# Half the columns of one block of the first modulation, on 40 partitions and in eight transfers of their own

## The chip, the cores and the metric

The kernel runs on one core of one Trainium2 chip. The metric is device time of one execution in microseconds (us). Five engines work side by side: TensorE (PE, with its weight loads as PEld), VectorE (DVE), ScalarE (ACT), GpSimd (POOL) and SyncE (SP), which here does nothing but issue transfers. Sixteen transfer engines (DMA) move data between the chip's memory (HBM) and the on-chip buffer of 128 partitions.

## The reference

One decode step of a transformer block with adaptive layernorm, for one token of width 640, all in float32:

```python
mod = (_silu(c) @ w_mod).reshape(c.shape[0], 6, 1, -1)
sa, ca, ga, sb, cb, gb = (mod[:, 0], mod[:, 1], mod[:, 2], mod[:, 3], mod[:, 4], mod[:, 5])
h = _layernorm(x, axis=-1) * (1 + ca) + sa
x = x + ga * _A_ref(h, A_k_cache, A_v_cache, A_wq, A_wo)
h = _layernorm(x, axis=-1) * (1 + cb) + sb
x = x + gb * _B_ref(h, B_w1, B_b1, B_w2, B_b2)
```

`_A_ref` is attention of one query over a cache: 32 heads of 192, 8192 positions. Keys and values are 32 x 8192 x 192 words each, 403 MB together, and make up nearly all that is read. `_B_ref` is a dense layer of 1536 with a squared relu. The first modulation, `sa` and `ca`, is a product of the 640 values of silu(c) with 640 x 1280 weights; without it there is no `h`, and without `h` no query.

## The kernel before, in words

**The stream.** A planner (`plan`, L50) cuts keys, values, the query weights and the output weights into 53 chunks of at most 84 x 192 = 16128 words a partition. Three buffers (`slot`, L97) take the chunks in turn; the first of them holds `wm0_t` (L113) at first, the weights of the first modulation, the first 512 columns of the query weights and the small vectors x, c, b1 and b2. After the chunks come the weights of the later modulations and of the dense layer. All loads are issued by SP, in the order of the program. `wm0_t` comes first (L114), then chunk 0 and chunk 1 (L222, L223), then chunk 2 when `wm0_t`'s buffer is free (L361), and from then on chunk n + 3 at the end of the work on chunk n (L410). A load is issued when its buffer is free. SP takes its instructions in order: one that waits holds those behind it.

**Completion.** In the built program each transfer announces its end on one of eight semaphores, which are given out in turn: the first to the eighth transfer have one each, the ninth has the first one's again. A transfer that takes a semaphore over waits until the earlier transfer with it has landed. In the kernel before the ninth transfer is chunk 7.

**The start.** When `wm0_t` has landed, DVE copies the small vectors (L117), ACT and DVE work out silu(c) (L168 to L171), and `mod` (L175) multiplies. The 640 rows of the weights are split into four groups of 160; each group is 5 blocks of 32 rows, and a group's 32 rows lie on 32 partitions. So block b of all four groups lies on 128 partitions, 2 x 640 words a block, and `mod` sums over the five blocks in one accumulator: 5 blocks x 4 matmuls (L183), each for 160 of the 640 columns of both `sa` and `ca`. The result is laid out by partition (L225), the layernorm of x follows (L232), and `query` (L235) makes the first 512 columns of the query (L246).

**A chunk** (L363 to L410): values times softmax weights on PE (L307), keys times query on DVE (L258), half of the additions on POOL (L385), sums to scores on DVE (L266), softmax where a head is complete (L277).

**The end.** The last output weights, the second modulation (`mod` again, L421), the gate, the second layernorm and the dense layer (L438, L453), and the store of 640 words (L458).

Of the kernel before, what the change touches and what calls it, by code (L numbers as in the profile page):

```python
# [8 lines left out]
F32 = mybir.dt.float32  # L9
# [4 lines left out]
P = 128  # L14
D = 640
# [4 lines left out]
G = 4  # L20
DG = D // G
FG = FF // G
KB = DG // 32
FB = FG // 32
# [12 lines left out]
WQ = KB * QC  # L37
UNIT = E * DH
EXTRA = {"o": WO, "q": WQ}
SLOT = 84 * DH  # L40
VPC = 5
LEAD_FROM = 1300
LEAD = 120
# [6 lines left out]
def plan():  # L50

    chunks, kp, vp, q, o = [], 0, 0, 1, 0
    while kp < H * NPOS or vp < H * NPOS // E:
        room, w = SLOT, []
        if o < NPAIR - 1 and 2 * (o + 1) * NPOS // E <= vp:
# [8 lines left out]
        else:  # L64
            v = VPC - 1 if kp >= LEAD_FROM else VPC
            nk = min(H * NPOS - kp, (room - v * UNIT) // DH)
# [14 lines left out]
def width(chunk):  # L81
    return chunk[1] * DH + chunk[3] * UNIT + sum(EXTRA[t] for t, _ in chunk[4])
# [3 lines left out]


@with_exitstack
def block_kernel(ctx: ExitStack, tc: tile.TileContext, kv, wm0, wm1, w1, w2, out):
    nc = tc.nc  # L90
    const = ctx.enter_context(tc.tile_pool(name="const", bufs=1))
    strm = ctx.enter_context(tc.tile_pool(name="strm", bufs=3))
# [4 lines left out]
    def slot(name):  # L97
        return strm.tile([P, SLOT], F32, tag="slot", name=name, bufs=3)

# [11 lines left out]
    nc.vector.memset(eps_t, EPS)  # L111

    wm0_t = slot("wm0_t")  # L113
    nc.sync.dma_start(wm0_t[:, :wm0.shape[1]], wm0)  # L114

    small = const.tile([P, 2 * KB + FB + KB], F32, name="small")
    nc.vector.tensor_copy(small, wm0_t[:, KB * 2 * D + WQ:wm0.shape[1]])  # L117
    x_c, c_c, bbc = small[:, :KB], small[:, KB:2 * KB], small[:, 2 * KB:]

    def columns(src, n, name, pool=const, **how):  # L120

        t = pool.tile([P, n // 32, 32], F32, name=name, **how)
        nc.vector.transpose(t.rearrange("p b r -> p (b r)"), src)
        return t
# [39 lines left out]
        return h  # L164


    e = const.tile([P, KB], F32, name="silu")
    nc.scalar.activation(e, c_c, AF.Exp, scale=-1.0)  # L168
    nc.vector.tensor_scalar(e, e, 1.0, None, op0=ALU.add)
    nc.vector.reciprocal(e, e)  # L170
# [1 line left out]

    mods = const.tile([P, 6, DG], F32, name="mods")

    def mod(first, n, w, between=lambda: None):  # L175

        ps = psum.tile([P, 512], F32, tag="q", name=f"ps_mod{first}", bufs=2)
        for b in range(KB):
            if b == 3:
                between()  # L180
            wb = w[:, b].rearrange("p (m n) -> p m n", m=n)
            for g in range(G):
                nc.tensor.matmul(ps[32 * g:32 * (g + 1), :n * DG], e[:, b:b + 1].to_broadcast([P, 32]),  # L183
                                 wb[:, :, DG * g:DG * (g + 1)], start=(b == 0), stop=(b == KB - 1))
        nc.vector.tensor_copy(mods[:, first:first + n], ps[:, :n * DG].rearrange("p (m n) -> p m n", m=n))

    def gate(m, w, steps):
# [16 lines left out]
    start = [sum(width(c) for c in PLAN[:n]) * P for n in range(len(PLAN))]  # L204

    def load(n):
        if n < len(PLAN):
            chunk_t[n] = slot(f"chunk{n}")
            m = width(PLAN[n])
            cuts = (m,) if n + 1 < len(PLAN) else ((PLAN[n][3] + 1) // 2 * UNIT, m)  # L210
            pieces = [(kv[start[n]:start[n] + P * m].rearrange("(p n) -> p n", p=P), cuts)]
        else:
            name, src, cuts = (("wm1_t", wm1, WM_CUT), ("w1_t", w1, W1_CUT), ("w2_t", w2, W2_CUT))[n - len(PLAN)]
            chunk_t[name] = slot(name)
            n, pieces = name, [(src, cuts)]
        for src, cuts in pieces:
            a = 0
            for b in cuts:
                nc.sync.dma_start(chunk_t[n][:, a:b], src[:, a:b])
                a = b  # L220

    load(0)  # L222
    load(1)  # L223
    mod(0, 2, wm0_t[:, :KB * 2 * D].rearrange("p (b n) -> p b n", b=KB))
    ma = columns(mods[:, 0:2].rearrange("p m n -> p (m n)"), 2 * DG, "ma")  # L225
    ca1 = const.tile([P, KB], F32, name="ca1")

# [7 lines left out]
    def query(u, w):  # L235
        w = w.rearrange("p (b n) -> p b n", b=KB)
        ps = psum.tile([P, 512], F32, tag="q", name=f"ps_q{u}", bufs=2)
        for b in range(KB):
            nc.tensor.matmul(ps, h1[:, b:b + 1].to_broadcast([P, P]), w[:, b], start=(b == 0), stop=(b == KB - 1))  # L239
        nc.scalar.activation(qb[:, QC * u % RING:QC * u % RING + QC], ps, AF.Copy, scale=DH ** -0.5)  # L240
# [2 lines left out]
    att_a = psum.tile([P, 512], F32, tag="att", name="att_a")  # L243
    att_s = const.tile([P, D], F32, name="att_s")
    nc.vector.memset(att_s, 0.0)
    query(0, wm0_t[:, KB * 2 * D:KB * 2 * D + WQ])  # L246

    sc = const.tile([P, SRING], F32, name="sc")

# [83 lines left out]
    def attend(i, w):  # L333
        oT = os_t.pop(i)
        w = w.rearrange("p (j n) -> p j n", j=NV)
        first, last = i == 0, i == NPAIR - 1
        oW = work.tile([P, NV, 32], F32, tag="oW", name=f"oW{i}")
        nc.scalar.activation(oW, oT[:, :, None].to_broadcast([P, NV, 32]), AF.Copy)  # L338
        for j in range(NV):
            nc.tensor.matmul(att_a[96:, :512], oT[:, j:j + 1].to_broadcast([P, 32]), w[:, j, :512],  # L340
                             start=(first and j == 0), stop=(last and j == NV - 1))
        nc.tensor.matmul(att_a[:96, :NV * (D - 512)], oW.rearrange("p j r -> p (j r)"), w[:, :, 512:],  # L342
                         start=first, stop=last)
# [19 lines left out]
    for n, (kp, nk, vp, nv, extra) in enumerate(PLAN):  # L363
# [3 lines left out]
        at = nk * DH + nv * UNIT  # L367
        wo_t = None
        for what, k in extra:
            w = t[:, at:at + EXTRA[what]]  # L370
# [10 lines left out]
        if nk:  # L381
            multiply(kt, kp, nk)
            m = nk - POOL * nk // 16
# [28 lines left out]
    wm1_t, w1_t, w2_t = chunk_t["wm1_t"], chunk_t["w1_t"], chunk_t["w2_t"]  # L412
# [5 lines left out]
        evict(h)  # L418
    turn(NPAIR - 1)
    attend(*wo_t)  # L420
    mod(2, 3, wm1_t[:, KB * D:KB * 4 * D].rearrange("p (b n) -> p b n", b=KB), gather)  # L421
    x1 = const.tile([P, DG], F32, name="x1")
    nc.vector.tensor_mul(x1, att_t[0][:, :DG], mods[:, 2])
    nc.vector.tensor_add(x1, x1, x_t)
# [11 lines left out]
    for b in range(KB):  # L436
        for g in range(G):
            nc.tensor.matmul(pf[32 * g:32 * (g + 1), :FG], hT2[:, b], w1_t[:, b, FG * g:FG * (g + 1)],  # L438
                             start=(b == 0), stop=(b == KB - 1))
# [11 lines left out]
    for b in range(FB):  # L451
        for g in range(G):
            nc.tensor.matmul(py[32 * g:32 * (g + 1), :DG], fT[:, b], w2_t[:, b, DG * g:DG * (g + 1)],  # L453
                             start=(b == 0), stop=(b == FB - 1))
# [46 lines left out]
```

## Time and profile before

| | |
|---|---|
| median of 3 runs | 1055.79 us (1055.74 to 1055.89) |
| the profiled execution | 1055.83 us, span 1054.0 us |
| DVE busy | 830.2 us, 79% |
| PE busy | 497.1 us, 47% |
| first weights (4493.5 KB) | issued at 0.74 us, 13.9 us to landing |
| first chunk (6144 KB) | issued at 1.19 us, 27.9 us to landing |
| first modulation on PE | 15.73 us to 20.74 us |
| first multiply on DVE | from 32.51 us |

The span is the part of the execution that the profiler sees, from the first instruction to the last; its times start at the span's start. A line of a view names the engine, the line of the kernel (L12), the operation, and what it writes and reads; in brackets stands how long the engine was idle before and what released it. "DMA to landing" is the time from a transfer's issue to the arrival of its last byte. Most of SP's waiting, and of every engine but the one that is late, costs nothing.

### The profile page before, as it was taken

Reading aid. Unit: us, or ns where it says so; the run is one execution under the profiler, and the core shown is the slowest. Engines: PE = TensorE matmul, PEld = TensorE weight load, DVE = VectorE, ACT = ScalarE, POOL = GpSimd, SP = SyncE. Lnnn points to the kernel's source line nnn. Section 1 sums busy time; section 2 is a strip of 40 time slices with the busy share of each in tenths; the row PEclk is TensorE's granted clock in tenths of the full one; section 3 lists DMA queues with packets and bytes.
Section 4 is the critical chain, followed back from the end, with each engine's and each line's share of the span. In section 5 each row is a group of like instructions: output and inputs, shape, how many; then the busy total and the mean of one; then the engine's idle time right before and its main releaser. Section 6 shows DMA issues by size and latency. Waiting matters only on the chain.

```text
span 1054.0 us, 5116 instructions
## 1 busy us (share of the span) xinstructions
PE 497.1 (47%) x2100; PEld 133.9 (13%) x2100; DVE 830.2 (79%) x428; ACT 43.5 (4%) x122; POOL 188.2 (18%) x57
## 2 busy tenths in 40 slices
PE   2253345565452364535354357344436346345286
PEld 1010011111110010101011011011001011011022
DVE  1798878877959969888797895999887977988822
ACT  1000000000000000000000000000000000000001
POOL 0212121121212202212121121122211211211200
PEclk9676576778666686668676577676677767768699
DMA  9999999999999999999999999999999999999997
GB/s 408 434 429 431 429 432 443 449 428 431 429 433 431 429 436 430 433 430 442 435 430 433 433 427 430 436 439 436 429 429 433 432 436 438 434 431 430 420 428 313
DMA packets 8960, 452.15 MB, mean 429 GB/s; under 512 B 997, under 2 KB 1001, under 8 KB 1129
## 3 DMA queue, kind: packets, MB, share of 16 engines
q1 hardware_dynamic: 8936, 451.83, 99.3%
q8 instruction: 16, 0.26, 0.1%
q14 instruction: 8, 0.06, 0.0%
HBM read 451.82 MB, written 0.00 MB: 429 GB/s over the span
## 4 chain that ended last, share of the span: by engine, by line
DMA 56%; DVE 30%; PE 12%; ACT 1%; issue 0%; SPq 0%; DVEq 0%
DMA chunk<-in_kv 53%; DVE chunk L258 16%; DVE sc L266 12%; PE ps_o L307 6%; PE ps_q L239 2%; DMA w_t<-in_w 2%; PE att_a L340 2%; DMA wm_t<-in_wm 1%; DVE os L321 1%; DVE om L319 1%; PE ps_mod L183 0%; PE att_a L342 0%; ACT p L290 0%; PE ps_mx L282 0%; DVE nm L284 0%
## 5 line engine op out<-in xcount | busy, mean ns | idle before, releaser
L258 DVE TENSOR_TENSOR chunk<-chunk,qb 128x8064 f32<-128x8064 f32 (+19 forms) x81 | 419.7, 5212 | 127.8 <-DMA chunk<-in_kv 122.5
L307 PE MATMUL ps_o<-chunk,p 128*32 128x512 f32 x1536 | 301.5, 747 | 70.3 <-DMA chunk<-in_kv 60.8
L266 DVE TENSOR_REDUCE sc<-chunk 128x25 f32<-128x4800 f32 (+21 forms) x109 | 333.9, 3097 | 0.4
L385 POOL TENSOR_TENSOR chunk<-chunk 128x1824 f32<-128x1824 f32 (+9 forms) x51 | 187.5, 3676 | 806.5 <-DVE chunk L258 578.5
L282 PE MATMUL ps_mx<-ident,mp 128*128 128x128 f32 x32 | 14.5, 452 | 346.8 <-DVE mp L280 346.8
L307 PEld LDWEIGHTS ps_o<-chunk,p 128*32 128x32 f32 x1536 | 68.2, 133 | 278.6 <-issue 193.1
L340 PE MATMUL att_a<-chunk,oT 128*32 128x512 f32 x96 | 65.1, 833 | 42.6 <-DVE oT L330 42.6
L239 PE MATMUL ps_q<-chunk,ln_h 128*128 128x512 f32 x110 | 66.6, 767 | 25.8 <-DMA chunk<-in_kv 25.8
L282 PEld LDWEIGHTS ps_mx<-ident,mp 128*128 128x128 f32 x32 | 5.6, 176 | 375.6 <-DVE mp L280 306.8
L290 ACT ACTIVATE p<-sc,nm 128x256 f32<-128x256 f32 x32 | 16.2, 508 | 649.6 <-DVE nm L284 649.6
L239 PEld LDWEIGHTS ps_q<-chunk,ln_h 128*128 128x128 f32 x110 | 26.7, 253 | 63.7 <-issue 34.6
L319 DVE TENSOR_TENSOR om<-ps_o,mask 96x512 f32<-96x512 f32 x32 | 21.6, 675 | 8.5 <-PE ps_o L307 8.5
L284 DVE TENSOR_REDUCE nm<-ps_mx 128x1 f32<-128x128 f32 x32 | 9.3, 292 | 19.5 <-PE ps_mx L282 19.5
L321 DVE TENSOR_REDUCE os<-om 96x64 f32<-96x512 f32 x32 | 21.8, 682 | 1.1
L340 PEld LDWEIGHTS att_a<-chunk,oT 128*32 128x32 f32 x96 | 12.2, 142 | 78.1 <-DVE oT L330 45.1
L329 DVE TENSOR_REDUCE oT<-ps_oT 128x3 f32<-128x96 f32 x16 | 4.0, 248 | 21.0 <-PE ps_oT L325 21.0
L295 PE MATMUL ps_sum<-ident,wide 128*128 128x128 f32 x16 | 7.4, 465 | 22.4 <-ACT wide L293 22.4
L183 PE MATMUL ps_mod<-wm_t,silu 128*32 128x320 f32 (+1 forms) x80 | 9.4, 621 | 15.8 <-DVE silu L171 15.7
L325 PE MATMUL ps_oT<-ident,os 96*128 96x96 f32 x16 | 5.0, 313 | 20.8 <-DVE os L321 20.8
L342 PE MATMUL att_a<-chunk,oW 128*96 128x384 f32 x32 | 14.6, 538 | 0.0
L240 ACT ACTIVATE qb<-ps_q 128x512 f32<-128x512 f32 x12 | 7.2, 597 | 137.2 <-PE ps_q L239 137.2
L338 ACT ACTIVATE oW<-oT 128x96 f32<-128x96 f32 x16 | 4.5, 280 | 177.6 <-DVE oT L330 177.6
(78 smaller groups left out, 93.6 us busy)
## 6 DMA issues: line engine op xcount, KB each, us to landing
chunk<-in_kv SPq DMA_DIRECT2D x38, 8064.0 KB, 37.2
chunk<-in_kv SPq DMA_DIRECT2D x11, 8000.0 KB, 39.0
chunk<-in_kv SPq DMA_DIRECT2D x2, 7872.0 KB, 38.5
chunk<-in_kv SPq DMA_DIRECT2D x1, 6144.0 KB, 27.9
wm_t<-in_wm SPq DMA_DIRECT2D x1, 4493.5 KB, 13.9
wm_t<-in_wm SPq DMA_DIRECT2D x1, 4480.0 KB, 27.6
chunk<-in_kv SPq DMA_DIRECT2D x1, 3264.0 KB
chunk<-in_kv SPq DMA_DIRECT2D x1, 3072.0 KB, 28.2
```

Source lines behind the costliest of these rows:

```text
L183: nc.tensor.matmul(ps[32 * g:32 * (g + 1), :n * DG], e[:, b:b + 1].to_broadcast([P, 32]), wb[:, :, DG * g:DG * (g + 1)], start=(b == 0), s ...
L239: nc.tensor.matmul(ps, h1[:, b:b + 1].to_broadcast([P, P]), w[:, b], start=(b == 0), stop=(b == KB - 1))
L258: nc.vector.tensor_mul(pr, pr, q[:, None, :].to_broadcast([P, b - a, DH]))
L266: nc.vector.tensor_reduce(sc[:, a % SRING:a % SRING + b - a], src[:, a - first:b - first], axis=AX.X, op=ALU.add)
L282: nc.tensor.transpose(ps[:, :P], mp.to_broadcast([P, P]), ident)
L290: nc.scalar.activation(p, s[:, :, None].to_broadcast([P, NPOS, 32 // E]), AF.Exp, bias=nm, accum_out=sp[:, h % 2:h % 2 + 1])
L307: nc.tensor.matmul(ps_t[h][32 * g:32 * (g + 1)], p[:, E * j:E * (j + 1)].rearrange("p e r -> p (e r)"), t[:, g], start=(j == 0), stop=last)
L319: nc.vector.tensor_mul(om[:n], ps_t.pop(h)[:n].rearrange("p (d e) -> p d e", e=E), mask[:n, None, :].to_broadcast([n, ED, E]))
L321: nc.vector.tensor_reduce(os_[:n, h % 2], om[:n], axis=AX.X, op=ALU.add)
L340: nc.tensor.matmul(att_a[96:, :512], oT[:, j:j + 1].to_broadcast([P, 32]), w[:, j, :512], start=(first and j == 0), stop=(last and j == NV ...
L342: nc.tensor.matmul(att_a[:96, :NV * (D - 512)], oW.rearrange("p j r -> p (j r)"), w[:, :, 512:], start=first, stop=last)
L385: nc.gpsimd.tensor_add(half, half, kt[:, m:, DH // 2:])
```

## The change

Block 4, the last of the five, is 2 x 640 words wide. Of it, the columns 320 to 639 of `sa` and of `ca` (`GX` = 2 of the 4 column groups, `WX` = 640 words) leave the rows of `wm0`. They lie in an array of their own, `wm0x`, of 40 rows, which go to partitions 0 to 19 and 32 to 51 (`RX` = 20). A row of it holds up to four (`SX`) pieces of 640 words: 128 rows of the block are dealt out over 40 partitions, 4 pieces on every fourth partition and 3 on the others. c is dealt out in the same way, in 4 more columns (`cx`).

The pieces come in eight transfers of five rows each, the rows of one transfer four partitions apart, 2560 words a row in the first of each four and 1920 in the others. They land at the end of the first buffer, on 64 partitions which DVE sets to zero first (partitions that hold no piece must be zero). `mod` does 18 of its 20 matmuls as before, and then 4 x 2 over 64 partitions, one for each piece and column group, with the matching column of silu(c). A row of `wm0` goes from 8987 to 8351 words (640 leave, 4 come).

In the built program the weights are the first transfer, the eight small ones the second to the ninth, and chunk 0 and chunk 1 the tenth and the eleventh. The ninth waits for the first one's semaphore. PE's first matmul on the pieces waits for all eight small transfers. Nothing else changes but the numbers of the lines.

```diff
+GX = 2
+SX = 4
+RX = 20
+WX = 2 * GX * DG
+W0 = KB * 2 * D - WX
...
     wm0_t = slot("wm0_t")
+    wm0x_t = wm0_t[:64, SLOT - SX * WX:]
+    nc.vector.memset(wm0x_t, 0.0)
     nc.sync.dma_start(wm0_t[:, :wm0.shape[1]], wm0)
+    for h in range(2):
+        for a in range(4):
+            n = WX * (SX if a == 0 else SX - 1)
+            nc.sync.dma_start(wm0x_t[32 * h + a:32 * h + RX:4, :n], wm0x[RX * h + a:RX * (h + 1):4, :n])
...
-    nc.vector.tensor_copy(small, wm0_t[:, KB * 2 * D + WQ:wm0.shape[1]])
-    x_c, c_c, bbc = small[:, :KB], small[:, KB:2 * KB], small[:, 2 * KB:]
+    nc.vector.tensor_copy(small, wm0_t[:, W0 + WQ:wm0.shape[1]])
+    x_c, c_c, bbc = small[:, :KB], small[:, KB:2 * KB + SX], small[:, 2 * KB + SX:]
...
-    def mod(first, n, w, between=lambda: None):
+    def mod(first, n, w, wx=None, between=lambda: None):
...
-            wb = w[:, b].rearrange("p (m n) -> p m n", m=n)
-            for g in range(G):
+            gs = G - GX if wx is not None and b == KB - 1 else G
+            wb = w[:, b * n * D:b * n * D + gs * n * DG].rearrange("p (m n) -> p m n", m=n)
+            for g in range(gs):
...
+        if wx is not None:
+            wx = wx.rearrange("p (s m n) -> p s m n", s=SX, m=n)
+            for s in range(SX):
+                for g in range(GX):
+                    nc.tensor.matmul(ps[32 * (G - GX + g):32 * (G - GX + g + 1), :n * DG],
+                                     e[:64, KB + s:KB + s + 1].to_broadcast([64, 32]),
+                                     wx[:, s, :, DG * g:DG * (g + 1)], start=False, stop=(s == SX - 1))
...
-    mod(0, 2, wm0_t[:, :KB * 2 * D].rearrange("p (b n) -> p b n", b=KB))
+    mod(0, 2, wm0_t[:, :W0], wm0x_t)
```

More of the change, by code (lines that the diff above doesn't have):

```diff
@@ L88, in block_kernel @@
 @with_exitstack
-def block_kernel(ctx: ExitStack, tc: tile.TileContext, kv, wm0, wm1, w1, w2, out):
+def block_kernel(ctx: ExitStack, tc: tile.TileContext, kv, wm0, wm0x, wm1, w1, w2, out):
     nc = tc.nc
@@ L113, in block_kernel @@
     wm0_t = slot("wm0_t")
+    wm0x_t = wm0_t[:64, SLOT - SX * WX:]
+    nc.vector.memset(wm0x_t, 0.0)
     nc.sync.dma_start(wm0_t[:, :wm0.shape[1]], wm0)
-    small = const.tile([P, 2 * KB + FB + KB], F32, name="small")
-    nc.vector.tensor_copy(small, wm0_t[:, KB * 2 * D + WQ:wm0.shape[1]])
-    x_c, c_c, bbc = small[:, :KB], small[:, KB:2 * KB], small[:, 2 * KB:]
+    for h in range(2):
+        for a in range(4):
+            n = WX * (SX if a == 0 else SX - 1)
+            nc.sync.dma_start(wm0x_t[32 * h + a:32 * h + RX:4, :n], wm0x[RX * h + a:RX * (h + 1):4, :n])
+    small = const.tile([P, 2 * KB + SX + FB + KB], F32, name="small")
+    nc.vector.tensor_copy(small, wm0_t[:, W0 + WQ:wm0.shape[1]])
+    x_c, c_c, bbc = small[:, :KB], small[:, KB:2 * KB + SX], small[:, 2 * KB + SX:]
     def columns(src, n, name, pool=const, **how):
@@ L164, in layernorm @@
         return h
-    e = const.tile([P, KB], F32, name="silu")
+    e = const.tile([P, KB + SX], F32, name="silu")
     nc.scalar.activation(e, c_c, AF.Exp, scale=-1.0)
@@ L245, in block_kernel @@
     nc.vector.memset(att_s, 0.0)
-    query(0, wm0_t[:, KB * 2 * D:KB * 2 * D + WQ])
+    query(0, wm0_t[:, W0:W0 + WQ])
     sc = const.tile([P, SRING], F32, name="sc")
@@ L420, in block_kernel @@
     attend(*wo_t)
-    mod(2, 3, wm1_t[:, KB * D:KB * 4 * D].rearrange("p (b n) -> p b n", b=KB), gather)
+    mod(2, 3, wm1_t[:, KB * D:KB * 4 * D], between=gather)
     x1 = const.tile([P, DG], F32, name="x1")
@@ L485 @@
           for kp, nk, vp, nv, extra in PLAN]
+    m0 = rows(wm[:, :2 * D], KB)
+    cc = column(c, KB)
+    at = [(s, 32 * h + r) for s in range(SX) for h in range(2) for r in range(RX) if s < SX - 1 or r % 4 == 0][:P]
+    xs, xp = np.array(at).T
+    xw, cx = np.zeros((P, SX, WX), np.float32), np.zeros((P, SX), np.float32)
+    xw[xp, xs] = m0[:, W0 - WX:].reshape(P, 2, D)[:, :, D - GX * DG:].reshape(P, WX)
+    cx[xp, xs] = cc[:, KB - 1]
     arrays = {
         "kv": np.concatenate(kv),
-        "wm0": np.concatenate([rows(wm[:, :2 * D], KB), wq[0], column(A_x, KB), column(c, KB),
-                               column(B_b1, FB), column(B_b2, KB)], axis=1),
+        "wm0": np.concatenate([m0[:, :W0 - WX], m0[:, W0 - WX:].reshape(P, 2, D)[:, :, :D - GX * DG].reshape(P, WX),
+                               wq[0], column(A_x, KB), cc, cx, column(B_b1, FB), column(B_b2, KB)], axis=1),
+        "wm0x": np.concatenate([xw[32 * h:32 * h + RX] for h in range(2)]).reshape(2 * RX, SX * WX),
         "wm1": np.concatenate([rows(wm[:, 5 * D:], KB), rows(wm[:, 2 * D:5 * D], KB)], axis=1),
```

## The prediction

> **What bounds the kernel now.** I read the page from the top first: the row of the sixteen transfer engines over the span, then the queues.
>
> ```profile
> span 1054.0 us, 5116 instructions
> DMA  9999999999999999999999999999999999999997
> q1 hardware_dynamic: 8936, 451.83, 99.3%
> HBM read 451.82 MB, written 0.00 MB: 429 GB/s over the span
> ```
>
> The queue that SP fills is busy for 99.3% of the span. No slice of the forty is below nine tenths but the last. The kernel is a stream of 452 MB, and its time is the time of that stream plus its two ends. The view of stretches says the same of the middle and shows the close.
>
> ```profile
> 55.00:1000.00 945.00, 443.72 (x1723) 115.08 (x1723) 788.36 (x367) 33.54 (x102) 181.60 (x50) 0.70 1.00 433
> 1040.00:1045.00 5.00, 2.37 (x32) 0.82 (x24) 2.43 (x6) 0.00 (x0) 0.00 (x0) 1.00 0.98 413
> 1045.00:1046.00 1.00, 0.60 (x20) 0.63 (x24) 0.15 (x1) 0.00 (x0) 0.00 (x0) 1.00 0.86 358
> 1047.00:1048.00 1.00, 0.24 (x8) 0.00 (x0) 0.00 (x0) 0.00 (x0) 0.00 (x0) 1.00 0.48 200
> 1049.00:1050.00 1.00, 0.74 (x24) 0.40 (x20) 0.00 (x0) 0.00 (x0) 0.00 (x0) 1.00 0.04 15
> ```
>
> The last two columns are the DMA share and GB/s. From 55 to 1000 us the share is 1.00 at 433 GB/s: nothing starves the engines. At the close the share falls over some four us, so the engines do not end together, and the last one sets the end. The chain of waits names compute as well, so I check that slots do not set the pace.
>
> ```profile
> DMA 56%; DVE 30%; PE 12%; ACT 1%; issue 0%; SPq 0%; DVEq 0%
> 45.51 10.22 DVE sc L266 x2
> 55.75 31.91 DMA chunk<-in_kv
> 1029.56 20.33 DMA w_t<-in_w
> ```
>
> The load issued at 55.75, when the scores of the first chunk free its slot, lands 31.91 us later. It is a full slot, 8064 KB, and its own bytes take 8.26 MB / 433 GB/s = 19.1 us. So 12.8 us of earlier transfers stood ahead of it. DVE's part of the chain is real, but it ends 12.8 us before the engines would run dry. A delay of the stream is thus a delay of the end. A delay of DVE is nothing until it reaches 12.8 us. The last transfer lands at 1029.56 + 20.33 = 1049.9, and only some 4 us of compute and the store follow.
>
> **The start, where the change lies.** The view in order of time (start, duration, engine, line) and the landings of the issues:
>
> ```profile
> 0.74 0.39 SPq L114 DMA_DIRECT2D wm_t<-in_wm  x1
> 1.19 31.01 SPq L219 DMA_DIRECT2D chunk<-in_kv  x3
> 1.64 0.06 DVE L111 MEMSET eps_t<- 128x1 f32 x1
> 14.62 0.18 DVE L117 COPY small<-wm_t 128x27 f32<-128x27 f32 x1 [12.92 <-DMA wm_t<-in_wm]
> 15.73 4.96 PE L183 MATMUL ps_mod<-wm_t,silu 128*32 128x320 f32 x40 [15.73 <-DVE silu L171]
> 24.47 7.38 PE L239 MATMUL ps_q<-wm_t,ln_h 128*128 128x512 f32 x10 [1.08 <-DVE ln_h L163]
> 32.51 12.96 DVE L258 TENSOR_TENSOR chunk<-chunk,qb 128x12288 f32<-128x12288 f32 x1 [5.34 <-ACT qb L240]
> chunk<-in_kv SPq DMA_DIRECT2D x1, 6144.0 KB, 27.9
> wm_t<-in_wm SPq DMA_DIRECT2D x1, 4493.5 KB, 13.9
> ```
>
> SP issues the first weights at 0.74, the first chunk right behind them at 1.19, and then the second. The weights land at 14.6 (DVE's copy runs at 14.62), the first chunk (6144 KB) at 1.19 + 27.9 = 29.1. Between the two landings 6.29 MB moved in 14.5 us: 434 GB/s. At that rate the weights' 4.60 MB are worth 10.6 us, but they took 13.9 from their issue. So a transfer that finds the engines empty pays **3.3 us of start-up** (issue, first bytes, the slowest engine's lag, the landing), and one that finds a queue pays none. This number carries the forecast.
>
> **The change part by part.**
>
> *The first transfer shrinks.* Its row goes from 8987 to 8351 words: 636 x 4 x 128 = 0.326 MB less, 0.75 us at 434 GB/s. It lands at 14.62 - 0.75 = 13.87.
>
> *Eight small transfers come behind it*, 2560 or 1920 words by five rows, 0.33 MB in all. The stream's bytes stay the same, so bytes cost nothing. The first of the eight waits for the new memset of 64 x 2560 words.
>
> ```profile
> 0.83 0.17 DVE L104 MEMSET ones<- 128x128 f32 x1 [0.83 <-PEq L494]
> 24.49 0.59 DVE L245 MEMSET att_s<- 128x640 f32 x1
> ```
>
> From 128 to 640 words a row, a memset grows by 0.42 us, 0.82 ns a word. 2560 words make 2.2 us, from 1.7 to 3.9. DVE has nothing else until 13.87, and the queue holds 0.33 MB less than 4.6 MB of work, so this is hidden. If that cover were gone it would cost 2.2 us. Between the two issues above lie 1.19 - 0.74 = 0.45 us, so seven small ones leave SP by 3.9 + 7 x 0.45 = 7.1, with the weights still under way.
>
> *The ninth transfer waits, and the chunks stand behind it.* The order of the built program gives every transfer one of eight semaphores in turn. The last small transfer is the ninth of the program and takes the first one's semaphore, so SP holds it until the weights have wholly landed. SP works in order: the first and the second chunk, which in the kernel before were issued by 1.19 and just after, are held behind it. This is a wait that the trace of before does not have, since there the ninth transfer comes long after the first. SP resumes at 13.87, issues the small one (0.45) and then the first chunk at 13.87 + 0.45 = **14.32**. By then the engines have drained: all that was queued is the weights, landed, and the seven small ones. The first chunk finds (nearly) empty engines, pays the start-up again, and lands at 14.32 + 3.3 + 14.5 = 32.1 where it landed at 29.1: **+3.0 us**, for it and everything behind it.
>
> This cost I bound from both sides. The start-up is 3.3 by the nearest row, a load over all partitions into empty engines. From below, the store at the end is the only other transfer that meets empty engines:
>
> ```profile
> 1051.47 0.65 SPq L458 DMA_DIRECT2D out_y<-y  x1
> SPq L497 <- DMA out_y<-y: 0.7, 1, 0.7
> ```
>
> It is issued for 0.65 us and waited for another 0.7: some 1.4 us for 2.5 KB on few engines. With 1.4 the sum is 14.32 + 1.4 + 14.5 - 29.1 = +1.1, with 3.3 it is +3.0. I take the nearest row's end, less a little, **+2.8**: part of the 3.3 is the lag of the slowest engine, and the close shows that the engines end four us apart, so the one that lags at the restart need not be the one that ends last. Upwards, a landing a few tenths later would add as much: up to +3.7.
>
> The Trainium skill (DMA: Bandwidth & Descriptors, section Anatomy of one DMA) gives a fixed cost of about 2.0 us for each transfer, fitted on GpSimd's path; that would make the sum +1.7, and the 3.3 us of this trace's own first load speaks for more.
>
> *The small rows' engines.* If five rows use five engines, each takes 2 x 10240 + 5 x 7680 = 58,880 bytes of the seven, 2.2 us at 434 / 16 = 27 GB/s. That ends by 13.87 + 2.2 = 16.1 at the latest, inside the start-up of the chunk (14.32 + 3.3), so it adds nothing.
>
> *More matmuls.* The modulation has 18 of the old and 8 new matmuls in place of 20; each counts twice in the row (x40), so 12 more at 4.96 / 40 = 0.124 us: +1.5 us on PE. The weights come 0.75 earlier, so the query and the first multiply move by about +0.7, to 33.2. The chunk, landing at 32.1, still comes before that. The slot then frees at some 56.5 and not 55.75, against 12.8 us of queue (and the stream is late itself), so nothing of it reaches the end. The last small transfer is issued at 13.87 and with 3.3 lands by 17.2; PE starts at 13.87 + (15.73 - 14.62) = 15.0 and reaches its rows 36 x 0.124 = 4.5 us later, at 19.5: hidden with 2.3 us to spare.
>
> *The sum.* The profiled execution took 1055.83 us, 1.8 more than its span, and the median of the runs is 1055.79, the same for this purpose. 1055.8 + 2.8 = **1058.6**.
>
> **The rivals.**
>
> *Slots absorb it.* If the loads wait for slots, and not for engines, a late stream catches up and only PE's +0.7 stays: 1056.5. For it speaks SP's own list of waits:
>
> ```profile
> SPq L219 <- DVE sc L266: 750.9, 50, 24.8
> chunk<-in_kv SPq DMA_DIRECT2D x38, 8064.0 KB, 37.2
> ```
>
> SP does wait 750.9 us for slots. Against it: the loads land 37.2 us after issue where their bytes take 19.1, so a full transfer stands ahead of each, and the share is 1.00 in the middle.
>
> *The slowest engines are unloaded.* This is the other side: not slower. The engines that carry no small row lose 0.75 us of work each, and if one of them ends last (the close runs over four us), the end comes 0.75 earlier: 1055.0. The Trainium skill (same page, sections Why a DMA increments its semaphore by 16 and not by 1, and The descriptor swizzle) says that five rows go to the five lowest engines and that partitions 0 to 19 and 32 to 51 are these engines' own, which would make this the effect; no row here names an engine. It decides only if the chunk is queued before the engines drain: by the sum above the shift is (start-up - 0.3), so the start-up would have to be under 0.3 us.
>
> *All five rows go through one engine.* Then one engine has 0.33 MB / 27 GB/s = 12 us more, the chunk's part on it starts some 10 us late, and the end with it: 1066. No row shows a five-row transfer.
>
> **How the numbers follow.** About 0.2% (2.1 us, so beyond 1057.9) is what a measurement of this kernel can tell from no change. The forecast, drained and refilled engines, has 0.80, between 1057.0 and 1059.5: 0.66 beyond 1057.9 and 0.14 short of it. Slots absorb it: 0.07. Unloaded engines: 0.06, one hundredth of that faster by over 0.2%. One engine: 0.04. What I have not thought of: 0.03, mostly slower. So slower 0.66 + 0.04 + 0.02 = 0.72, faster 0.02, within 0.2% the remaining 0.26. The bounds +1.1 and +3.7 make the range 1057.0 to 1059.5, which leaves the three rivals out.
>
> **What would show it.** In the profile after, DVE's copy of the small columns should start near 13.9; SP's first chunk issue should stand near 14.3, not 1.19, with a wait for the first weights ahead of it; the DMA share between about 14 and 16 should fall well below one; the multiply should start near 33.2 with the chunk just landed; from 55 to 1000 the share should be 1.00 again. If the chunk is issued by 8 us, the forecast is wrong and the unloaded engines are next. If the share in the middle falls below 1.00, slots do set the pace.

## The result and the profile after

| | before | after |
|---|---|---|
| median of 9 runs | 1055.79 us (1055.62 to 1056.00) | 1058.68 us (1058.49 to 1058.87) |
| ratio | | 1.0026 (95%: 1.0017 to 1.0035) |
| the profiled execution, its span | 1055.83 us, 1054.0 us | 1058.74 us, 1057.0 us |

The change costs 2.9 us, 0.26%. The forecast was 1058.6. Where the time went is read in the same order as before. First the page of the kernel after, its span, the engines' row over the span, and SP's queue:

```profile
span 1057.0 us, 5161 instructions
DMA  8999999999999999999999999999999999999997
q1 hardware_dynamic: 9016, 451.83, 99.1%
```

The bytes are the same 451.83 MB. Of the forty slices one has changed: the first, from 9 to 8. The view in order of time of the kernel after shows what happens in that slice:

```profile
2.17 2.19 DVE L120 MEMSET wm_t<- 64x2560 f32 x1 [0.48 <-issue]
4.39 9.66 SPq L125 DMA_DIRECT2D wm_t<-in_wm0x  x8
13.40 0.18 DVE L128 COPY small<-wm_t 128x31 f32<-128x31 f32 x1 [9.03 <-DMA wm_t<-in_wm]
14.09 17.65 SPq L238 DMA_DIRECT2D chunk<-in_kv  x3
14.54 4.68 PE L195 MATMUL ps_mod<-wm_t,silu 128*32 128x320 f32 x36 [14.54 <-DVE silu L182]
19.15 2.34 PE L201 MATMUL ps_mod<-wm_t,silu 64*32 64x320 f32 x16
25.25 6.13 PE L258 MATMUL ps_q<-wm_t,ln_h 128*128 128x512 f32 x10 [1.08 <-DVE ln_h L174]
32.05 12.96 DVE L277 TENSOR_TENSOR chunk<-chunk,qb 128x12288 f32<-128x12288 f32 x1 [4.09 <-ACT qb L259]
```

The first chunk is issued at 14.09 and not at 1.19. It goes out 0.69 us after the weights have landed (13.40). The eight small transfers leave SP between 4.39 and 14.05, and the one row for the eight hides a gap before the last. SP's waits in the kernel after (what it waited for: us in total, times, the longest) name that gap:

```profile
SPq L125 <- DMA wm_t<-in_wm: 3.9, 1, 3.9
SPq L125 <- DVE wm_t L120: 3.3, 1, 3.3
```

Once, SP waits for the memset, and once, for 3.9 us, for the first weights: the ninth transfer, held by the first one's semaphore. The stretches of the kernel after (the last two columns are the DMA share and GB/s; a packet is booked where it begins, so a stretch can exceed 1):

```profile
12.00:13.00 1.00, 0.00 (x0) 0.00 (x0) 0.00 (x0) 0.00 (x0) 0.00 (x0) 1.00 0.24 97
13.00:14.00 1.00, 0.00 (x0) 0.00 (x0) 0.32 (x2) 0.37 (x2) 0.00 (x0) 1.00 0.33 136
14.00:15.00 1.00, 0.46 (x4) 0.20 (x8) 0.42 (x3) 1.00 (x1) 0.00 (x0) 1.00 0.26 92
15.00:16.00 1.00, 1.00 (x12) 0.40 (x8) 0.00 (x0) 0.13 (x1) 0.00 (x0) 1.00 2.39 745
20.00:30.00 10.00, 7.01 (x24) 3.18 (x21) 4.81 (x16) 0.26 (x1) 0.00 (x0) 0.83 0.95 413
55.00:1000.00 945.00, 435.73 (x1722) 112.95 (x1722) 786.07 (x366) 33.53 (x102) 181.53 (x50) 0.71 1.00 433
```

In the kernel before, the same stretches read:

```profile
12.00:13.00 1.00, 0.00 (x0) 0.00 (x0) 0.00 (x0) 0.00 (x0) 0.00 (x0) 1.00 0.36 157
13.00:14.00 1.00, 0.00 (x0) 0.00 (x0) 0.00 (x0) 0.00 (x0) 0.00 (x0) 1.00 1.48 639
14.00:15.00 1.00, 0.00 (x0) 0.00 (x0) 0.18 (x1) 0.16 (x1) 0.00 (x0) 1.00 0.80 344
20.00:30.00 10.00, 6.98 (x23) 3.13 (x16) 4.82 (x16) 0.26 (x1) 0.00 (x0) 0.67 1.01 436
```

From 13 to 15 us the engines were at work before (1.48 and 0.80); after, they stand mostly idle (0.33 and 0.26) and the chunk's packets come in the stretch from 15 (2.39). Counted from the trace's single packets, the sixteen engines stand idle for some 32 engine-us between 12 and 16 us, 2.0 us each; in the kernel before they are never idle there. The restart is slow as well: the eight packets of the first chunk that an engine carries take 15.2 us together, where they took 14.5. The last packets of the first chunk end at 30.26 to 31.38 on the sixteen engines, where they ended at 27.56 to 28.75, 2.8 us later on the mean: 2.0 of idle engines and 0.7 of slower packets make nearly all of it. Then the share is 1.00 at 433 GB/s from 55 to 1000, as before: nothing of the delay is caught up and nothing is added, and the end comes 2.9 us later.

### The profile page after: what moved, and what is told of

It reads as the page before. It is cut to its first block, busy times and chain, and to the rows that moved or that the text cites. A ratio compares the mean times of both kernels' runs of the same rounds, so it can differ in the third digit from the quotient of the medians.

```text
span 1057.0 us, 5161 instructions
## 1 busy us (share of the span) xinstructions
PE 491.0 (46%) x2112; PEld 133.1 (13%) x2112; DVE 832.6 (79%) x429; ACT 43.5 (4%) x122; POOL 188.1 (18%) x57
## 3 DMA queue, kind: packets, MB, share of 16 engines
q1 hardware_dynamic: 9016, 451.83, 99.1%
HBM read 451.83 MB, written 0.00 MB: 427 GB/s over the span
## 4 chain that ended last, share of the span: by engine, by line
DMA 56%; DVE 31%; PE 11%; ACT 1%; issue 0%; SPq 0%; DVEq 0%
DMA chunk<-in_kv 53%; DVE chunk L277 16%; DVE sc L285 13%; PE ps_o L326 5%; PE att_a L359 2%; DMA w_t<-in_w 2%; PE ps_q L258 2%; DMA wm_t<-in_wm 1%; DVE os L340 1%; DVE om L338 1%; PE att_a L361 0%; ACT p L309 0%; PE ps_mx L301 0%; PE ps_mod L195 0%; DVE nm L303 0%
## 5 line engine op out<-in xcount | busy, mean ns | idle before, releaser
L326 PE MATMUL ps_o<-chunk,p 128*32 128x512 f32 x1536 | 296.5, 735 | 79.1 <-DMA chunk<-in_kv 69.4
L258 PE MATMUL ps_q<-chunk,ln_h 128*128 128x512 f32 x110 | 63.4, 735 | 26.4 <-DMA chunk<-in_kv 26.4
L195 PE MATMUL ps_mod<-wm_t,silu 128*32 128x480 f32 (+1 forms) x76 | 9.1, 615 | 15.2 <-DVE silu L182 14.5
L361 PE MATMUL att_a<-chunk,oW 128*96 128x384 f32 x32 | 14.5, 534 | 0.0
```

What stands on the lines that cost most here:

```text
L326: nc.tensor.matmul(ps_t[h][32 * g:32 * (g + 1)], p[:, E * j:E * (j + 1)].rearrange("p e r -> p (e r)"), t[:, g], start=(j == 0), stop=last)
```

## The experiments

The theory was that the ninth transfer's wait empties the engines and that the refill costs some 3 us, whatever the small transfers carry. The rivals were the bytes on few engines, the mere number of transfers and a late DVE. The intervals of the ratios below are some ±0.9 us wide, so two kernels less than 1 us apart are not told apart by them.

### Six or seven unread transfers in the kernel before

Into the kernel before, between the weights and the first chunk, go six (e3) or seven (e4) transfers of five rows by 128 words that nobody reads. With seven, the first chunk is the ninth transfer.

```diff
     nc.sync.dma_start(wm0_t[:, :wm0.shape[1]], wm0)
+    for i in range(6):     # e4: range(7)
+        nc.sync.dma_start(wm0_t[:5, SLOT - P * (i + 1):SLOT - P * i], wm0[:5, P * i:P * (i + 1)])
```

> The kernel before with six transfers of five rows of 512 bytes, that nobody reads, between the weights and the first chunk; the first chunk is the eighth transfer and does not wait. Theory: 1055.8, within 0.3, since the issue of the first chunk at some 4 us is still far ahead of the drained engines. Rival (small transfers cost in themselves): +0.45 us for each, 1058.5.

> The same with seven: the first chunk is the ninth transfer and waits for the weights, which land at 14.6. Theory: issue at some 14.65, 0.56 later than in the change, so the loss is 2.9 + 0.56 = 3.4 us: 1059.2 (1058.8 to 1059.6). Rival (small transfers cost in themselves): 0.45 more than with six.

Measured: e3 1056.16 us, ratio 1.0004 (0.9995 to 1.0013). e4 1059.03 us, 1.0030 (1.0019 to 1.0042), so +3.2. In order of time, e3:

```profile
1.19 2.19 SPq L116 DMA_DIRECT2D wm_t<-in_wm  x6
3.42 28.51 SPq L221 DMA_DIRECT2D chunk<-in_kv  x3
```

and e4:

```profile
1.18 2.64 SPq L116 DMA_DIRECT2D wm_t<-in_wm  x7
14.32 0.18 DVE L119 COPY small<-wm_t 128x27 f32<-128x27 f32 x1 [12.63 <-DMA wm_t<-in_wm]
14.32 18.02 SPq L221 DMA_DIRECT2D chunk<-in_kv  x3
```

In e4 the chunk's issue and the copy stand at the same 14.32: both waited for the weights. SP's waits in e4 name it:

```profile
SPq L221 <- DMA wm_t<-in_wm: 10.5, 1, 10.5
```

and the stretches of e4 show empty engines:

```profile
13.00:14.00 1.00, 0.00 (x0) 0.00 (x0) 0.00 (x0) 0.00 (x0) 0.00 (x0) 1.00 0.09 18
14.00:15.00 1.00, 0.00 (x0) 0.00 (x0) 0.37 (x3) 0.44 (x2) 0.00 (x0) 1.00 0.00 0
```

What follows: the step from six to seven transfers of 2.5 KB costs 2.9 us (1059.03 - 1056.16). Between the two neither matmuls nor a memset has changed, and of the bytes only 2.5 KB. The wait alone is enough for the whole of the change's cost, and six transfers without it cost nothing that can be measured.

### Seven unread transfers, one of them ahead of the weights

If the wait for the weights costs, and not the reuse of a semaphore as such, it must go when a tiny transfer has the first semaphore. One transfer is issued ahead of the weights, the other six behind them; they have 1, 2, 3, 4, 5 and 5 rows.

```diff
+    def mark(rows, n, at):
+        nc.sync.dma_start(wm0_t[:rows, SLOT - at - n:SLOT - at], wm0[:rows, at:at + n])
+
+    mark(5, P, 0)
     nc.sync.dma_start(wm0_t[:, :wm0.shape[1]], wm0)
+    for i, rows in enumerate((1, 2, 3, 4, 5, 5)):
+        mark(rows, P * (i + 2), P * (i + 1) * (i + 2) // 2)
```

> The kernel before with seven unread marks, as many as in the run that lost 3.2 us, but one of them ahead of the weights, and with one to five rows. The first chunk is the ninth transfer and waits for that first mark, which lands at some 2.5 us, so it is issued with the weights under way. Theory (what counts is what the wait is for): 1055.8 plus 0.4, as the weights are issued one mark later: 1056.2 (1055.9 to 1056.6). Rival (the number of transfers or the re-used semaphore itself): 1059.0 as with seven marks behind the weights.

Measured: 1057.18 us, 1.0011 (1.0003 to 1.0020), +1.3. In order of time:

```profile
3.85 12.25 SPq L225 DMA_DIRECT2D chunk<-in_kv  x2
15.76 0.18 DVE L123 COPY small<-wm_t 128x27 f32<-128x27 f32 x1 [14.06 <-DMA wm_t<-in_wm]
```

The chunk is issued at 3.85 with the engines full, so the ninth transfer now waits for nothing that is late, and 1.9 of the 3.2 us are gone. But 1.3 us stay where 0.4 was expected. The weights, issued at 1.19, land at 15.76: 15.76 - 1.19 - 10.6 of bytes leaves 4.0 us of start-up, 0.7 more than before. That and 0.45 us for the later issue would make 1.15. Why this start-up is longer is not shown.

### The change with six small transfers

The change itself, but with five pieces in the longest rows and so three transfers for each half: six in all, and the first chunk is the eighth transfer.

```diff
-SX = 4
+SX = 5
...
-        for a in range(4):
+        for a in range(3):
...
```

The array `wm0x` is filled to match.

> The change with six small transfers in place of eight (three of each four partitions, up to five pieces on a partition), so that the first chunk is the eighth transfer and waits for no semaphore; the second chunk waits for the weights with the first one queued behind them. Theory (the wait drained the engines): the first chunk's issue is back near 8 us, the engines are not idle between 13 and 15, and the 2.9 us of the change go. What stays is the moved bytes: five engines carry 1.7 us more (2.4 of small rows less 0.75), eleven 0.75 less. If one of the eleven ends last as in the rival of the prediction, 1055.0; if one of the five does, up to 1057.3. Rival (the small transfers or the matmuls themselves cost): 1058.2 to 1058.8 as the change.

Measured: 1057.37 us, 1.0015 (1.0006 to 1.0024), +1.6. In order of time the chunk leaves early and the weights land at 13.7:

```profile
9.46 4.57 SPq L238 DMA_DIRECT2D chunk<-in_kv  x2
13.70 0.18 DVE L128 COPY small<-wm_t 128x32 f32<-128x32 f32 x1 [8.67 <-DMA wm_t<-in_wm]
```

The stretches of e1 around that landing:

```profile
13.00:14.00 1.00, 0.00 (x0) 0.00 (x0) 0.18 (x1) 0.08 (x1) 0.00 (x0) 1.00 0.52 214
14.00:15.00 1.00, 0.16 (x4) 0.16 (x8) 0.56 (x3) 0.98 (x2) 0.00 (x0) 1.00 1.84 791
```

The wait ahead of the first chunk is gone and the engines do not run dry (a packet is booked where it begins, hence 0.52 beside 1.84; counted from the single packets no engine is idle between 12 and 16 us), yet half of the cost is left. It shows at the other end of the kernel, in the last stretches:

```profile
1047.00:1048.00 1.00, 1.00 (x20) 0.86 (x16) 0.00 (x0) 0.00 (x0) 0.00 (x0) 0.50 0.52 215
1048.00:1049.00 1.00, 1.00 (x23) 0.84 (x16) 0.00 (x0) 0.00 (x0) 0.00 (x0) 0.50 0.09 36
1049.00:1050.00 1.00, 1.00 (x30) 0.78 (x26) 0.00 (x0) 0.00 (x0) 0.00 (x0) 0.75 0.06 26
1050.00:1051.00 1.00, 0.98 (x32) 0.64 (x20) 0.00 (x0) 0.00 (x0) 0.00 (x0) 1.00 0.04 15
```

A share of 0.06 is one engine of sixteen, at 26 GB/s. In the kernel before the stretch from 1048 has five times that:

```profile
1048.00:1049.00 1.00, 0.62 (x20) 0.60 (x24) 0.00 (x0) 0.00 (x0) 0.00 (x0) 1.00 0.30 123
```

There several engines shared the end; here a single one works alone from 1048.4 to 1050.8. The trace does not name the engines, but each packet begins 3 or 4 ns before the end of its predecessor on the same engine. Followed so, packet by packet, it is one of the five that carry small rows. The other four end at 1046.8 to 1047.9. This one also fetches instructions: four short fetches, and each of them delays its other packets by 0.98 us, 3.9 us together. In the kernel before the engine with these four fetches ended at 1049.2 already, beside eight engines with two longer fetches each (1.5 to 1.6 us of delay for one, ends at 1047.9 to 1049.45). Its small rows put it behind all of them: it carries 2 x 12,800 + 4 x 10,240 bytes and loses 8 x 635 x 4 of the weights' rows, 46,240 bytes more, 1.7 us at 27 GB/s.

So when the stream does not stop, the bytes do cost, on one engine. When it stops, as in the change, the five engines move their small rows while the other eleven stand idle, and the price is not paid on top: 2.9 for both, 3.2 for the wait alone (in e4), 1.6 for the bytes without the wait. The first two are not told apart. The packets of the kernel after agree: the engine with the four fetches ends at 1052.2, the next one, which carries no small row, at 1052.0.

### Six small transfers, with more and with fewer bytes

Three runs vary what the engines carry. e6 has six transfers of four rows (`SX = 6`, `RX = 16`). e10 moves half the bytes (`GX = 1`, the edits of `SX` and of the loop as in e1). e2 moves all of the block's columns (`GX = 4`).

> The six small transfers with four rows in place of five (24 partitions, up to six pieces each), so that four engines carry the rows: each 3.0 us more less 0.75. In the trace of the six transfers by five rows, followed engine by engine, one of the five ends last and the other four end with some 3 us to spare, since that one also carries four short instruction fetches. If that engine is the fifth, it is spared here and the eleven others and it lose 0.75: 1055.0 to 1055.3. If it is one of the first four: 2.3 more than before, less what it has to spare: 1057.8 to 1058.1.

> The six small transfers by five rows with one column group and not two: rows half as long, so each of the five engines carries 1.2 us more less 0.37, 0.85 in place of 1.7. Theory (the five engines' bytes are what is left when the wait is gone): the excess is about half of the 1.57 us measured with two groups, 1056.4 to 1056.7. Rival (the six transfers, the memset or the matmuls): as with two groups, 1057.4.

> As the six transfers, with all four column groups of the last block and not two: the small rows are twice as long, so the five engines carry 3.3 us more and the eleven 1.5 less. Unloaded engines: 1054.3. Five engines that end last: the excess over before is twice that of the six transfers with half the block, some +3 us, 1058.9. Rival (neither matters): the same as the six transfers with half the block.

Measured: e6 1057.90 us, 1.0018 (1.0009 to 1.0027), +2.0. e10 1057.08 us, 1.0012 (1.0003 to 1.0021), +1.2. e2 1060.32 us, 1.0044 (1.0031 to 1.0056), +4.5. The close of e6:

```profile
1049.00:1050.00 1.00, 1.00 (x20) 0.85 (x16) 0.00 (x0) 0.00 (x0) 0.00 (x0) 0.50 0.05 20
1050.00:1051.00 1.00, 1.00 (x21) 0.82 (x17) 0.00 (x0) 0.00 (x0) 0.00 (x0) 0.56 0.06 26
```

and of e10:

```profile
1048.00:1049.00 1.00, 1.00 (x24) 1.00 (x19) 0.00 (x0) 0.00 (x0) 0.00 (x0) 0.50 0.05 20
1049.00:1050.00 1.00, 1.00 (x20) 0.53 (x16) 0.00 (x0) 0.00 (x0) 0.00 (x0) 0.50 0.07 31
```

In both, one engine is alone again, and it is among the loaded, in e6 too with four rows a transfer. By the working of e1, a loaded engine carries 23,200 bytes more in e10 (0.9 us), 46,240 in e1 (1.7) and 61,632 in e6 (2.3); measured were +1.2, +1.6 and +2.0. The order is right, the slope is not settled, since each pair's intervals overlap. In all three the late engine is the one with the four fetches; its last packet, at 1049.2 in the kernel before, ends at 1050.6 in e10, 1050.8 in e1 and 1051.6 in e6.

e2 does not answer what it was made for. Its order in time shows why:

```profile
2.97 5.39 DVE L121 MEMSET wm_t<- 64x6400 f32 x1 [1.27 <-issue]
8.39 4.38 SPq L126 DMA_DIRECT2D wm_t<-in_wm0x  x6
12.81 0.44 SPq L241 DMA_DIRECT2D chunk<-in_kv  x1
```

The memset is 5.39 us long and SP waits for it, six issues follow, and the chunk goes out at 12.81, after the weights have landed (12.75). The engines ran dry here too, 29.6 engine-us idle between 12 and 16 us, though no semaphore held the chunk: a memset ahead of the issues is enough when it is long. Its +4.5 us mixes this with the bytes.

### The pieces on 32 partitions, in one transfer

One transfer of 32 rows onto partitions 0 to 31 brings the same 128 pieces. There is neither a memset nor a ninth transfer.

```diff
-RX = 20
+RX = 32
...
-    wm0x_t = wm0_t[:64, SLOT - SX * WX:]
-    nc.vector.memset(wm0x_t, 0.0)
+    wm0x_t = wm0_t[:RX, SLOT - SX * WX:]
...
-    for h in range(2):
-        for a in range(4):
-            n = WX * (SX if a == 0 else SX - 1)
-            nc.sync.dma_start(wm0x_t[32 * h + a:32 * h + RX:4, :n], wm0x[RX * h + a:RX * (h + 1):4, :n])
+    nc.sync.dma_start(wm0x_t, wm0x)
...
```

> The change with its 128 pieces on 32 partitions (four each, 0 to 31) in one transfer of 32 rows, two rows for each of sixteen engines, and no memset. No wait ahead of the first chunk and no engine with more bytes than another; the eight extra matmuls stay. Theory: 1055.8, within 0.3. Rival (the matmuls, or the small rows themselves, cost): over 1056.5.

Measured: 1057.01 us, 1.0010 (1.0001 to 1.0018), +1.1 where nothing was expected, though the interval hardly separates it from nothing. The order in time has nothing late:

```profile
1.20 0.41 SPq L121 DMA_DIRECT2D wm_t<-in_wm0x  x1
1.65 30.18 SPq L234 DMA_DIRECT2D chunk<-in_kv  x3
14.06 0.18 DVE L124 COPY small<-wm_t 128x31 f32<-128x31 f32 x1 [12.36 <-DMA wm_t<-in_wm]
```

The trace's packets hold a hint. The small rows are packets of 10,240 bytes; in the change those take 0.385 us each, here 0.385 to 0.922, with a median of 0.664. At two rows for each of sixteen engines that is some 0.6 us. The first chunk's packets behind them are slower too (15.5 us an engine for 14.5), and its last ones end at 29.12 to 29.95, 1.6 us later on the mean than before, with no engine idle between 12 and 16 us. So the loss is made in the transfers at the start; in e1, which has more extra matmuls, those packets take 14.5. That many engines writing few partitions at once slow each other is a guess, and the cause of this 1.1 us stays open.

### A late DVE

In the kernel before, the memset of `att_s` that stands in front of the first multiply is repeated, 14, 20 or 25 times in all. Only DVE is late then, by 0.79 us for each memset and gap, less what it would have waited for the query.

```diff
-    nc.vector.memset(att_s, 0.0)
+    for _ in range(25):     # e9: 20, e12: 14
+        nc.vector.memset(att_s, 0.0)
```

> The kernel before with 14 memsets in place of one ahead of the first multiply, so that it starts near 37.6, some 5 us late. In the run with 20 (9.8 late) the load was issued at 65.5, the DMA rate between 65 and 70 fell to 361 GB/s, and 1.9 us were lost: so the queue ahead was not 12.8 us long but that less the start-up, 12.8 - 3.3 = 9.5. Theory (9.5 us cover a late DVE): 1055.8, within 0.4, and no dip between 60 and 70. Rival (DVE's lateness costs in proportion, 1.9 us for 9.8): 1056.8.

> The kernel before with 20 memsets in place of one ahead of the first multiply. In the run with 25 each took 0.79 us with its gap, so the multiply started at 46.45, 13.9 us late and not 9.6 as expected, past the 12.8 us of queued transfers, and the DMA share fell to 0.48 between 60 and 70 us. With 20 it starts near 42.5, 10.0 late, and the load that follows is issued 2.8 us ahead of dry engines. Theory: 1055.8, within 0.5. Rival (a late DVE costs its share from the first us): 1055.8 + 5.1 x 10.0 / 13.9 = 1059.5.

> The kernel before with 25 memsets of 0.59 us in place of one before the first multiply, which then starts near 42 and not 32.5. Theory (12.8 us of queued transfers cover a late DVE): 1055.8, within 0.4. Rival (slots set the pace): up to 9.6 us more, 1065.

Measured: e12 1055.98 us, 1.0001 (0.9992 to 1.0010); e9 1057.80 us, 1.0021 (1.0013 to 1.0030), +1.9; e8 1061.04 us, 1.0048 (1.0034 to 1.0062), +5.1. The first multiply starts at 37.48, 42.32 and 46.45 us, so 5.0, 9.8 and 13.9 late. The stretch from 65 to 70 us, in which the queued transfers come to their end and the next should follow, in e12:

```profile
65.00:70.00 5.00, 5.00 (x27) 1.65 (x28) 4.97 (x2) 0.60 (x1) 2.03 (x1) 1.00 0.95 413
```

in e9:

```profile
65.00:70.00 5.00, 4.12 (x6) 1.97 (x7) 4.34 (x4) 0.60 (x2) 0.00 (x0) 0.50 0.98 361
```

and in e8:

```profile
65.00:70.00 5.00, 0.00 (x0) 0.02 (x1) 4.83 (x3) 0.00 (x0) 0.32 (x1) 0.50 0.00 0
```

413, 361 and 0 GB/s: fed, short, and dry. A DVE that is 5 us late is free: counted from the single packets, no engine of e12 is idle between 55 and 80 us. At 9.8 late it costs 1.9 and at 13.9 late 5.1. If every us beyond the cover costs one, the cover is some 9.8 - 1.9 = 7.9 to 13.9 - 5.1 = 8.8 us. The packets give it more sharply: the engines stand idle for 0.9 us each in e9 and 5.0 us each in e8, and 9.8 - 0.9 and 13.9 - 5.0 are both 8.9.

### The price of an issue over stepped partitions

The small transfers of the change left SP more slowly than forecast. e11 is e3 with the rows four partitions apart.

```diff
-        nc.sync.dma_start(wm0_t[:5, SLOT - P * (i + 1):SLOT - P * i], wm0[:5, P * i:P * (i + 1)])
+        nc.sync.dma_start(wm0_t[:20:4, SLOT - P * (i + 1):SLOT - P * i], wm0[:5, P * i:P * (i + 1)])
```

> The six unread marks behind the weights, 512 bytes a row, on partitions 0, 4, 8, 12, 16 and not 0 to 4. In the change each small transfer held SP for 0.66 us, the marks for 0.33. If the step of the partitions makes the difference: 0.66 us each here; if the length of the rows: 0.33. The time stays that of the six marks, 1056.2 (1055.7 to 1056.6), since the first chunk is still issued by 6 us.

Measured: 1056.02 us, 1.0001 (0.9992 to 1.0010). The views of the one line (duration in ns: least, median, most; then the first and the last start) of e3:

```profile
L116 SPq DMA_DIRECT2D wm_t<-in_wm x6: 262/323/403, 1.2 to 3.0; - x6
```

of e11:

```profile
L116 SPq DMA_DIRECT2D wm_t<-in_wm x6: 657/657/856, 1.2 to 4.9; - x6
```

and of the kernel after:

```profile
L125 SPq DMA_DIRECT2D wm_t<-in_wm0x x8: 657/658/867, 4.4 to 13.4; - x8
```

Five rows on neighbouring partitions are issued in 0.32 us, five rows four partitions apart in 0.66, and the change pays the latter. In e11, and for the first seven transfers of the change, nothing of it reaches the end, since SP is ahead of the engines there.

## Why the prediction was right

*The stream sets the end.* Right. Chunk 0 is 2.8 us late on the mean engine, the end 2.9, and the share between is 1.00. The cover that the prediction put beside it, 12.8 us for a late DVE, was **too large**: e9 loses 1.9 us at 9.8 late, and by the packets the cover is 8.9. The packets show the two parts that the working missed. In the kernel before, the load issued at 55.75 begins at 65.8 on the mean engine, so the work queued ahead lasts 10.0 us and not 12.8. The 12.8 was taken from the landing at 87.66, and the slowest engine sets that: its packets end at 87.2, those of the mean engine at 84.9. And a late load, in e8 issued at 69.64, has its first packet at 70.60, 1.0 us later: 10.0 - 1.0 = 9.0. The change did not come near this bound.

*The weights shrink.* They landed at 13.40, not 13.87. Without their 9.85 us of bytes and the issue at 0.73 this leaves 2.8 us of start-up, where the first load before had 3.3.

*Memset and issues.* The memset was sized right (2.19 us for 2.2). The issues were not: 0.66 us each, not 0.45, as the nearest row had been a transfer over neighbouring partitions and e11 shows that the step makes the difference. Seven left by some 9.5 us and not 7.1; SP then still waited 3.9 us for the weights, so this did not count. The ninth, behind the landing, did count its 0.69 (with the gap) instead of 0.45.

*The ninth transfer's wait and the refill.* This is the step that carries the sum, and e3 against e4 shows it alone: nothing for six, 2.9 us for one more. e7 shows from the other side that it is the wait for the weights. The chunk's issue came at 14.09 (forecast 14.32), two errors that nearly cancel: 0.47 earlier landing, 0.24 longer issue. From there its last packet ends at 31.38, 31.38 - 14.09 - 14.5 = 2.8 us of start-up; 1.1 of it passes before the first packet (15.18). The prediction's 3.3 counts to the landing, which in the kernel before came 0.3 after the last packet (29.1 against 28.75); counted so, the restart is some 3.1, inside the bounds of 1.4 and 3.3 and close to the upper. The Trainium skill (DMA: Bandwidth & Descriptors, Anatomy of one DMA) has some 2.0 us for a transfer's fixed cost, fitted on GpSimd's path. The restart here is above it, as the prediction had held. The last tenths are luck: the step gives +2.6 on the slowest engine, the mean engine is 2.8 late and the end 2.9, so the little that the prediction took off for the slowest engine is not borne out.

*The small rows' engines: nothing.* Right for the change, but with a reason that e1 narrows. The last of them end at 15.43 (forecast 16.1 at the latest). They are hidden because the engines stand idle; in e1, where these do not, one loaded engine ends last and the small rows cost 1.6 us.

*More matmuls.* PE's part of the modulation took 4.68 + 2.34 = 7.02 us for 4.96, so +2.1 and not +1.5: the passes over 64 partitions cost 2.34 / 16 = 0.146 us and not 0.124. Yet the multiply started at 32.05, earlier than before and than the 33.2 of the forecast, as the query took 6.13 us and not 7.38; the granted clock from 20 to 30 us was 0.83 where it was 0.67. Neither reaches the end.

*The rivals.* That slots absorb it was wrong: the share in the middle is 1.00, and the end is as late as the first chunk. That all five rows go through one engine was wrong: the trace shows five packets at a time, one on each of five engines (the first five begin between 12.28 and 12.51 us). The Trainium skill (DMA: Bandwidth & Descriptors, Why a DMA increments its semaphore by 16 and not by 1) gives five rows five engines, and the trace agrees. That the unloaded engines would end earlier fell in a way that the prediction did not have. Its condition, a chunk queued before the engines drain, was met in e1, and the unloaded engines did end earlier there, the last of them at 1048.4 where it was 1049.45. Yet the time came out 1.6 us above before and not 0.75 below: the engine that ends last was one of the loaded.

No version that was run is faster than the kernel before. The best that lighter unloaded engines could give, 0.75 us or 0.07%, is less than these runs can tell from nothing.

## What to carry to other kernels

Count the transfers ahead of the first large stream: where completions share a few semaphores in turn, one small transfer more can wait for the first large one, hold everything behind it in the same queue, and empty the engines. A refill is paid once in full by a kernel that the transfers bound. Cover for a late issue is the work still queued on the mean engine, less the time from an issue to its first packet (1.0 us here); a landing overstates it. Before giving bytes to a few engines, look at the last microseconds for the engine that ends last, and see that it is not among them.

## What the runs showed of the hardware that was not expected

- A transfer over stepped partitions keeps SP for 0.66 us, one of the same size over neighbouring ones for 0.32 (e11 and e3).
- The start-up of the first weights is not one number: 3.3 us before, 2.8 after, 4.0 in e7.
- The engines do not end alike because they do not carry alike: fetches of instructions ride on some of them. Two long ones delay each of eight engines by 1.5 to 1.6 us apiece, and four short ones delay the engine that ended last in e1 by 0.98 us apiece (kernel before and e1).
- Small rows onto 32 partitions from all engines at once took 0.664 us in the median for packets that took 0.385 from five engines (e5); why is open.
